# Attention and two MoE layers on one core: the slow widening of one weight unit, shared by VectorE, GpSimd and ScalarE

## The chip, the core and the metric

One core of a Trainium2 chip runs the whole program in one launch. The metric is the device time of that launch in microseconds (us); the kernel before has a median of 787.21 us over three runs (786.08 to 787.22). VectorE is written DVE, ScalarE ACT, GpSimd POOL, TensorE PE, SyncE SP.

## What is computed

```python
def reference(**kwargs):
    attn_out = _attn_ref(q, k, v)             # rotary, softmax(q k^T / 8), times v; (2, 8, 576, 64)
    x = attn_out.transpose(0, 2, 1, 3).reshape(1152, 512)
    x = _moe_ref(x, w_in, w_out)              # silu(x @ w_in) @ w_out, d_ff 2048
    return _moe2_ref(x, domain_probs, w1, w2) # 4 experts: sum_e p_e * relu(x @ w1[e]) @ w2[e]
```

`moe_w_in` and `moe_w_out` come as 8-byte floats. The kernel reads each of them as two 32-bit words, a low word and a high word, and has to build from them a pair of 4-byte tiles whose sum stands for the weight: `wh`, what TensorE multiplies with directly, and `wl`, the rest. Each product is then three matmuls (`wh*xh`, `wh*xl`, `wl*xh`).

## The kernel before

**Attention** works on 8 pairs of heads. A pair has 9 units of work, so that the loop at L1104 takes 72 steps; step i belongs to pair i // 9, and s = i % 9 is its place in the pair. What each step issues on each engine is written out by hand: `PLAN` (L15 to L17) says which background work of the neighbouring pairs falls on which s, and `ORDER` (L18 to L20) in which order a step issues scores (S), row maxima (M), exponentials (E), transposes (T), their evacuations (H on ACT, L on DVE), and the rest. Engines run what they were issued in this order and wait for each other through semaphores. From pair 6 on there is no second pair ahead any more, so that pairs 6 and 7 run by `PLAN2` and `ORDER2` and have no rotary work.

POOL has these steps in each of the pairs 0 to 5: the rotary of the pair after the next (`rotary_k` L232 to L241, `rotary_q` L251 to L267), the low part of V (`vsplit` L284, which waits for ACT's copy at L280), the row factors for the norm (`rbc`, L521 and L526) and the low part of the attention output (`xl`, L550, which waits for ACT's `xh` at L549, which waits for DVE's `xn` at L554).

**The weights.** `Feed` (L119) hands out the widening in stages: each call of `feed.tick` at the end of a step runs one stage of every slice that is under way, then starts another slice if it may (L169, steps in `CONV`, L21). Weight unit 0 (the first 512 columns of `w_in`) is widened during attention, in four slices of 128x512, by `slice0` (L997) with `slow=True`: the slice is loaded into `raw0`, of which there is a single buffer (L156), and then takes one stage in each of nine steps. Slices start at steps 15, 24, 33 and 51, all of them s = 6, so that they lie in pairs 2, 3, 4 and 6. All further units come after attention, or at its very end, in three stages a slice (L117), which the change leaves as they are.

One slice before: ACT takes the absolute value of the high word (t0, L88) and casts `wh` (t5, L104); DVE does the other seven operations (L89, L92, L95, L98, L101, L107, L110). Both words stand interleaved in `raw`, so that `lw` and `hw` are every second 32-bit word.

**The MoE layers** (L882) start in the last pair, run on the tiles `xh` and `xl`, and take the rest of the time.

Of the kernel before, what the change touches and what calls it, by code (L numbers as in the profile page):

```python
# [9 lines left out]
U32 = mybir.dt.uint32  # L10
AF = mybir.ActivationFunctionType
ALU = mybir.AluOpType
# [18 lines left out]
def f32(ap):  # L31
    return ap.bitcast(F32)
# [3 lines left out]
def fused_kernel(ctx, tc, q, k, v, w_in, w_out, dprobs, w1, w2, cst, out):  # L36
    nc = tc.nc
# [43 lines left out]
    def widen(cv, raw, wh, wl, slow=False):  # L81
        lw, hw = (raw.rearrange("p (n a) -> p n a", a=2)[:, :, a] for a in range(2))
        T = {}
        V = nc.vector

        def t0():
            T["t"] = t = cv.tile([128, 512], U32, name="cvt")
            nc.scalar.activation(f32(t), f32(hw), AF.Abs)  # L88
            V.tensor_scalar(lw, lw, 9, None, ALU.logical_shift_right)  # L89

        def t1():
            V.scalar_tensor_tensor(lw, hw, 23, lw, ALU.logical_shift_left, ALU.bitwise_or)  # L92

        def t2():
            V.tensor_scalar(f32(T["t"]), f32(T["t"]), 2.0 ** -15, None, ALU.max)  # L95

        def t3():
            V.tensor_scalar(T["t"][:], T["t"][:], 3, 0x3FFFF000, ALU.logical_shift_left, ALU.bitwise_and)  # L98

        def t4():  # L100
            V.scalar_tensor_tensor(T["t"][:], hw, 0xC0000000, T["t"][:], ALU.bitwise_and, ALU.bitwise_or)  # L101

        def t5():
            nc.scalar.copy(wh, f32(T["t"]))  # L104

        def t6():
            V.tensor_scalar(hw, T["t"][:], 0xFF800000, None, ALU.bitwise_and)  # L107

        def t7():
            V.scalar_tensor_tensor(wl, lw, 2.0 ** -43, f32(hw), ALU.mult, ALU.mult)  # L110

        def together(*fns):
            return lambda: [fn() for fn in fns]

        if slow:
            return [lambda: None, t0, t1, t2, t3, t4, t5, t6, t7]
        return [together(t0, t1), together(t2, t3, t4), together(t5, t6, t7)]  # L117

    class Feed:  # L119
# [722 lines left out]
    def queue(n):  # L842
        wh, wl = wslot[n % 4]
        raws = {}

        def conv(t):
            if t % 2 == 0:
                raws[0] = stg.tile([128, 2, 1024], U32, name="raw", tag="raw")
                nc.sync.dma_start(raws[0][:], units[n][:, t:t + 2, :])
            return widen(cv, raws[0][:, t % 2, :], wh[:, t, :], wl[:, t, :])  # L850

        for t in range(FT):
            feed.add(n, lambda t=t: conv(t))
# [115 lines left out]
    def attention():  # L969
# [27 lines left out]
        def slice0(t):  # L997
            raw = stg0.tile([128, 1024], U32, name="raw0")
            nc.sync.dma_start(raw[:], units[0][:, t, :])
            return widen(cv0, raw, wslot[0][0][:, t, :], wslot[0][1][:, t, :], True)  # L1000
# [274 lines left out]
```

## Time and profile before

| | us |
|---|---|
| median of three runs | 787.21 |
| the profiled execution | 785.77 |
| its span, first to last instruction | 784.0 |
| PE, DVE, ACT, POOL busy in the span | 749.1, 526.2, 349.8, 299.4 |

The profiled execution is 1.44 us below the median; 1.77 us of it lie around the span. A timeline row gives the start of an instruction (or of a run of equal ones, "x2"), its length, and in brackets how long its engine was idle before it and for whom. "POOL xl L550 <- ACT xh L549" says that POOL stood still until ACT had written `xh`. A row of the view by tile gives the shortest, median and longest length of one instruction in ns. The granted clock of TensorE is 0.991 of the full rate over the span and 1.00 in every stretch that is discussed here.

### The profile page before, as it was taken

Reading aid. Unit: us, or ns where it says so; the run is one execution under the profiler, and the core shown is the slowest. Engines: PE = TensorE matmul, PEld = TensorE weight load, DVE = VectorE, ACT = ScalarE, POOL = GpSimd, SP = SyncE. Lnnn points to the kernel's source line nnn. Section 1 sums busy time; section 2 is a strip of 40 time slices with the busy share of each in tenths; the row PEclk is TensorE's granted clock in tenths of the full one; section 3 lists DMA queues with packets and bytes.
Section 4 is the critical chain, followed back from the end, with each engine's and each line's share of the span. In section 5 each row is a group of like instructions: output and inputs, shape, how many; then the busy total and the mean of one; then the engine's idle time right before and its main releaser. Section 6 shows DMA issues by size and latency. Waiting matters only on the chain.

```text
span 784.0 us, 12147 instructions
## 1 busy us (share of the span) xinstructions
PE 749.1 (96%) x4592; PEld 693.9 (89%) x4592; DVE 526.2 (67%) x963; ACT 349.8 (45%) x837; POOL 299.4 (38%) x321
## 2 busy tenths in 40 slices
PE   4898898999999999999969999999999999999998
PEld 3897787989999999999969898988989889898996
DVE  6779998887999899894894454544545454354542
ACT  3788778885534525234443141322423234142320
POOL 8778667521001303105771523516134160432500
PEclk9899999999999999999989999999999999999999
DMA  4443543240313133131100120301103021030002
GB/s 127 117 127 83 127 127 89 63 129 11 103 60 109 54 108 108 55 109 53 54 19 37 42 66 1 108 1 55 55 0 109 0 56 52 3 106 1 1 28 94
DMA packets 30986, 51.89 MB, mean 66 GB/s; under 512 B 7168, under 2 KB 13968, under 8 KB 30928
## 3 DMA queue, kind: packets, MB, share of 16 engines
q1 hardware_dynamic: 28800, 50.06, 21.0%
q10 hardware_dynamic: 2000, 0.77, 0.4%
q8 instruction: 36, 0.59, 0.3%
q0 software_dynamic: 128, 0.28, 0.1%
q14 instruction: 22, 0.18, 0.1%
HBM read 41.40 MB, written 2.36 MB: 56 GB/s over the span
## 4 chain that ended last, share of the span: by engine, by line
PE 83%; DVE 9%; ACT 3%; DMA 2%; issue 1%; POOL 1%; ACTq 0%; DVEq 0%; POOLq 0%
PE m L817 9%; PE m L816 9%; PE m L818 9%; PE m L743 7%; PE m L745 7%; PE m L744 7%; PE m L639 4%; PE m L641 4%; PE m L640 4%; PE b L301 4%; PE b L501 4%; PE m L664 4%; PE m L662 4%; PE m L663 4%; PE s L396 3%; ACT p L425 2%
## 5 line engine op out<-in xcount | busy, mean ns | idle before, releaser
L822 DVE SCALAR_TENSOR_TENSOR acc<-m,dp,acc 128x512 f32<-128x512 f32 (+1 forms) x64 | 47.5, 743 | 112.3 <-PE m L818 112.3
L817 PE MATMUL m<-wl,gh 128*128 128x512 f32 (+1 forms) x292 | 114.6, 392 | 0.0
L818 PE MATMUL m<-wh,gl 128*128 128x512 f32 (+1 forms) x292 | 114.5, 392 | 0.0
L816 PE MATMUL m<-wh,gh 128*128 128x512 f32 (+1 forms) x292 | 114.5, 392 | 0.0
L764 DVE SCALAR_TENSOR_TENSOR gl<-g,gh 128x288 fp32r<-128x288 f32 x96 | 56.9, 593 | 49.1 <-ACT gh L763 48.5
L726 POOL TENSOR_TENSOR wl<-raw,wh 128x512 fp32r<-128x512 f32 x24 | 31.1, 1296 | 142.6 <-ACT wh L723 142.6
L651 POOL TENSOR_TENSOR gl<-g,gh 128x384 fp32r<-128x384 f32 x24 | 27.1, 1130 | 142.3 <-ACT gh L650 142.2
L743 PE MATMUL m<-xh,wh 128*128 128x288 f32 x256 | 76.1, 297 | 0.0
L745 PE MATMUL m<-xh,wl 128*128 128x288 f32 x256 | 75.7, 296 | 0.0
L744 PE MATMUL m<-xl,wh 128*128 128x288 f32 x256 | 75.7, 296 | 0.0
L726 POOL TENSOR_TENSOR wl<-cvt,wh 128x512 fp32r<-128x512 f32 x32 | 41.8, 1309 | 74.0 <-ACT wh L723 74.0
L663 PE MATMUL m<-gh,wl 128*128 128x384 f32 (+1 forms) x208 | 67.2, 323 | 0.0
L664 PE MATMUL m<-gl,wh 128*128 128x384 f32 (+1 forms) x208 | 67.2, 323 | 0.0
L662 PE MATMUL m<-gh,wh 128*128 128x384 f32 (+1 forms) x208 | 67.2, 323 | 0.0
L818 PEld LDWEIGHTS m<-wh,gl 128*128 128x128 f32 x292 | 54.8, 188 | 12.9
L816 PEld LDWEIGHTS m<-wh,gh 128*128 128x128 f32 x292 | 54.9, 188 | 11.9
L817 PEld LDWEIGHTS m<-wl,gh 128*128 128x128 f32 x292 | 54.8, 188 | 11.8
L743 PE MATMUL m<-tf,wh 128*128 128x288 f32 x192 | 57.4, 299 | 6.7 <-DVE g L798 5.6
L723 ACT CAST wh<-cvt 128x512 fp32r<-128x512 f32 x32 | 19.9, 620 | 96.3 <-DVE cvt L722 96.3
L301 PE MATMUL b<-cs,p 128*128 128x128 f32 x329 | 51.1, 286 | 11.0 <-ACT p L1018 7.1
L425 ACT ACTIVATE p<-s,nm 128x576 f32<-128x576 f32 x72 | 53.9, 749 | 9.2 <-DVE nm L415 8.5
L763 ACT ACTIVATE gh<-g 128x288 fp32r<-128x288 f32 x96 | 42.9, 447 | 33.6 <-DVE g L798 19.0
(174 smaller groups left out, 2124.3 us busy)
## 6 DMA issues: line engine op xcount, KB each, us to landing
raw<-in_moe_w_dram SPq DMA_DIRECT2D x16, 1024.0 KB, 5.2
raw<-in_moe_w_out_dram SPq DMA_DIRECT2D x8, 1024.0 KB, 4.9
raw<-in_moe_w_in_dram SPq DMA_DIRECT2D x6, 1024.0 KB, 5.0
kh<-kkh SPq DMA_DIRECT2D x28, 128.0 KB, 2.5
kl<-kkl SPq DMA_DIRECT2D x28, 128.0 KB, 2.4
xv<-in_v_dram SPq DMA_DIRECT2D x8, 256.0 KB, 2.8
raw<-in_moe_w_in_dram SPq DMA_DIRECT2D x4, 512.0 KB, 4.1
xk<-in_k_dram SPq DMA_DIRECT2D x7, 256.0 KB, 2.9
```

Source lines behind the costliest of these rows:

```text
L301: nc.tensor.matmul(o, lhsT, idn[:, 0:n], is_transpose=True, start=True, stop=True)
L425: nc.scalar.activation(o.rearrange("p (a b) -> p a b", a=2), s[:, :, 0:288], AF.Exp, bias=P.nm[:, c:c + 1], scale=1.0, accum_out=P.sm[:, c ...
L662: nc.tensor.matmul(o, wh[:, f, ds], gh[:, cols], start=(f == 0), stop=False)
L663: nc.tensor.matmul(o, wl[:, f, ds], gh[:, cols], start=False, stop=False)
L664: nc.tensor.matmul(o, wh[:, f, ds], gl[:, cols], start=False, stop=(f == FT - 1))
L726: nc.gpsimd.tensor_tensor(lo, src(name), f32(hi), ALU.subtract)
L743: nc.tensor.matmul(ps, wh[:, k, ms], hh[:, k, cols], start=(first and k == 0), stop=False, skip_group_check=not first)
L744: nc.tensor.matmul(ps, wh[:, k, ms], hl[:, k, cols], start=False, stop=False, skip_group_check=not first)
L745: nc.tensor.matmul(ps, wl[:, k, ms], hh[:, k, cols], start=False, stop=(k == 1), skip_group_check=not first)
L816: nc.tensor.matmul(ps, gh[:, ts], wh[:, f, ds], start=(f == 0), stop=False)
L817: nc.tensor.matmul(ps, gh[:, ts], wl[:, f, ds], start=False, stop=False)
L818: nc.tensor.matmul(ps, gl[:, ts], wh[:, f, ds], start=False, stop=(f == FT - 1))
```

## The change

Only the slow form of `widen` changes. New stages u0 to u8 stand beside the old ones; t4 (L101) is kept and called from u3.

```diff
+        def u0():
+            T["t"] = t = cv.tile([128, 512], U32, name="cvt")
+            nc.scalar.activation(f32(t), f32(hw), AF.Abs)
+        def u1():
+            nc.gpsimd.tensor_scalar(f32(T["t"]), f32(T["t"]), 2.0 ** -15, 0.0, ALU.max, ALU.max)
+        def u3():
+            nc.scalar.activation(f32(lw), lw, AF.Copy, scale=2.0 ** -52)
+            t4()
+        def u2():
+            V.tensor_scalar(T["t"][:], T["t"][:], 3, 0x3FFFFFFF, ALU.logical_shift_left, ALU.bitwise_and)
+        def u4():
+            V.tensor_scalar(hw, T["t"][:], 0xFF800000, None, ALU.bitwise_and)
+        def u5():
+            nc.gpsimd.tensor_tensor(f32(hw), f32(lw), f32(hw), ALU.mult)
+        def u6():
+            nc.gpsimd.tensor_tensor(f32(T["t"]), f32(T["t"]), f32(hw), ALU.add)
+        def u7():
+            nc.scalar.copy(wh, f32(T["t"]))
+        def u8():
+            nc.gpsimd.tensor_tensor(wl, f32(T["t"]), f32(wh), ALU.subtract)
         if slow:
-            return [lambda: None, t0, t1, t2, t3, t4, t5, t6, t7]
+            return [lambda: None, u0, u1, u2, u3, u4, u5, u6, u7, u8]
```

For a slice DVE goes from seven operations to three (u2, t4, u4), ACT from two to three (u0, u3, u7), POOL from none to four (u1, u5, u6, u8). There are ten stages instead of nine. Counted from a slice's start, u0 falls on s = 8, u1 on s = 0 of the next pair, u2 on 1, u3 with t4 on 2, u4 on 3, u5 on 4, u6 on 5, u7 on 6, u8 on 7. All other instructions keep their order; their line numbers are 29 higher in the changed kernel.

POOL in pair 2, s = 3 to s = 8, before (`yq` and `t_994` are the rotary's, `xl` the low part of the attention output, `rb` the row factors, `V` the low part of V):

```order
L251 TENSOR_TENSOR t_994<-xq,cs 128x576
L550 TENSOR_TENSOR xl<-xn,xh 128x320
L521 TENSOR_SCALAR rb<-rs 128x256
L254 TENSOR_TENSOR yq<-xq,cs 128x9x64
L258 TENSOR_TENSOR t_994<-t_994,yq 128x576
L264 TENSOR_SCALAR yq<-t_994 128x9x64
L267 TENSOR_TENSOR yq<-t_994,yq 128x9x64
L284 TENSOR_TENSOR V<-xv,V 128x4x64 x2
```

The same place of the changed kernel, from its `yq` of L283 (L254 before) on:

```order
L283 TENSOR_TENSOR yq<-xq,cs 128x9x64
L133 TENSOR_TENSOR raw_766<-raw_766 128x512
L287 TENSOR_TENSOR t_994<-t_994,yq 128x576
L136 TENSOR_TENSOR cvt<-cvt,raw_766 128x512
L293 TENSOR_SCALAR yq<-t_994 128x9x64
L296 TENSOR_TENSOR yq<-t_994,yq 128x9x64
L142 TENSOR_TENSOR wl_65<-cvt,wh_64 128x512
L313 TENSOR_TENSOR V<-xv,V 128x4x64 x2
```

u5 (L133) and u6 (L136) stand behind `xl`, `rb` and two rotary instructions of the same pair, and u8 (L142) behind the last of them.

ACT in pair 2, s = 6 to s = 8, in the changed kernel (`pth` are transposed probabilities, `p,sm` the exponentials, `tmp` a half of the output):

```order
L492 CAST pth<-b 128x4x128
L139 CAST wh_64<-cvt 128x512
L492 CAST pth<-b 128x4x128
L494 COPY p_999<-b 128x128
L454 ACTIVATE p,sm_111<-s,nm 128x576
L377 ACTIVATE Q<-b 128x512
L540 COPY tmp<-b 64x256
L454 ACTIVATE p,sm_112<-s,nm 128x576
L492 CAST pth<-b 128x4x2x64
L494 COPY p_999<-b 128x64
L309 CAST V<-xv 128x4x64 x2
L117 ACTIVATE cvt<-raw_1084 128x512
```

The cast of `wh`, u7 (L139), now stands here between two casts of `pth`, and it needs what POOL's u6 wrote; before, it stood in s = 4 behind the cast of `xh`, and needed DVE's L101.

## Rows read from the trace of the kernel before

**Rows 1.** Windows: stretch, us, then busy us of each engine, clock, DMA share, GB/s.
```profile
58.55:128.32 69.77, 61.00 (x441) 53.94 (x441) 65.71 (x112) 55.16 (x142) 48.14 (x54) 1.00 0.39 99
81.89:105.24 23.35, 20.18 (x148) 17.91 (x148) 21.62 (x38) 18.42 (x48) 16.05 (x19) 1.00 0.42 107
128.32:147.86 19.54, 19.22 (x148) 17.92 (x146) 15.48 (x30) 17.12 (x47) 15.30 (x20) 1.00 0.35 97
147.86:168.52 20.66, 19.75 (x149) 18.03 (x148) 19.45 (x38) 18.37 (x49) 4.92 (x9) 1.00 0.27 66
186.00:784.00 598.00, 587.63 (x3441) 547.87 (x3439) 368.26 (x686) 205.33 (x464) 180.37 (x165) 0.99 0.17 54
```
**Rows 2.** Instructions on tile raw, 57 to 170 us: ns min/median/max, first and last start.
```profile
L88 ACT ACTIVATE cvt<-raw x4: 678/688/702, 58.7 to 148.0; 128x512 f32<-128x512 f32 x4
L89 DVE TENSOR_SCALAR raw<-raw x4: 449/740/789, 59.5 to 148.8; 128x512 uint32<-128x512 uint32 x4
L92 DVE SCALAR_TENSOR_TENSOR raw<-raw x4: 681/888/905, 61.8 to 151.5; 128x512 uint32<-128x512 uint32 x4
L101 DVE SCALAR_TENSOR_TENSOR cvt<-raw,cvt x4: 658/910/1162, 70.1 to 159.0; 128x512 uint32<-128x512 uint32 x4
L107 DVE TENSOR_SCALAR raw<-cvt x4: 417/1584/1600, 74.5 to 163.0; 128x512 uint32<-128x512 uint32 x4
L110 DVE SCALAR_TENSOR_TENSOR wl<-raw x4: 681/1211/1212, 77.5 to 165.1; 128x512 fp32r<-128x512 uint32 x4
```
**Rows 3.** The same view of tile cvt.
```profile
L95 DVE TENSOR_SCALAR cvt<-cvt x4: 407/540/1033, 64.9 to 153.8; 128x512 f32<-128x512 f32 x4
L98 DVE TENSOR_SCALAR cvt<-cvt x4: 417/524/774, 67.1 to 156.7; 128x512 uint32<-128x512 uint32 x4
L104 ACT CAST wh<-cvt x4: 613/614/624, 71.6 to 159.7; 128x512 fp32r<-128x512 f32 x4
```
**Rows 4.** The chain that ended last, 78 to 210 us: start, us, what.
```profile
78.76 4.37 DMA raw<-in_moe_w_in_dram
...
102.10 4.12 DMA raw<-in_moe_w_in_dram
```
**Rows 5.** DVE, timeline: `xn` in pair 3 and in pair 5, and pair 5's longest stop.
```profile
94.05 0.47 DVE L554 TENSOR_TENSOR xn<-xu,b 128x320 f32<-128x320 f32 x1
...
135.98 0.49 DVE L513 TENSOR_TENSOR xu<-b,tmp 64x320 f32<-64x320 f32 x1 [1.29 <-ACT tmp L511]
...
138.20 0.46 DVE L554 TENSOR_TENSOR xn<-xu,b 128x320 f32<-128x320 f32 x1
```
**Rows 6.** POOL, timeline, pair 3.
```profile
81.89 1.43 POOL L284 TENSOR_TENSOR V<-xv,V 128x256 fp32r<-128x256 f32 x2 [3.71 <-ACT V L280]
...
84.18 1.27 POOL L232 TENSOR_TENSOR t<-xk,cs 128x512 f32<-128x512 f32 x1
...
88.53 1.48 POOL L232 TENSOR_TENSOR t<-xk,cs 128x512 f32<-128x512 f32 x1
...
95.09 0.86 POOL L550 TENSOR_TENSOR xl<-xn,xh 128x320 fp32r<-128x320 f32 x1 [1.51 <-ACT xh L549]
95.92 0.40 POOL L521 TENSOR_SCALAR rb<-rs 128x256 f32<-128x256 f32 x1
96.29 1.41 POOL L254 TENSOR_TENSOR yq<-xq,cs 128x576 f32<-128x576 f32 x1
97.78 1.42 POOL L258 TENSOR_TENSOR t<-t,yq 128x576 f32<-128x576 f32 x1
99.28 0.73 POOL L264 TENSOR_SCALAR yq<-t 128x576 fp32r<-128x576 f32 x1
```
**Rows 7.** ACT, timeline, pair 5, s = 6 to s = 8.
```profile
142.69 1.08 ACT L463 CAST pth<-b 128x512 fp32r<-128x512 f32 x2 [0.30 <-PE b L301]
...
145.67 0.36 ACT L511 COPY tmp<-b 64x256 f32<-64x256 f32 x1 [0.51 <-PE b L501]
...
147.35 0.73 ACT L280 CAST V<-xv 128x256 fp32r<-128x256 f32 x2
```

## The prediction

> **What bounds the kernel now.** I read the windows view first, by pairs of heads. The borders are the starts of POOL's low part of V (the two-instruction row at 81.89 in [rows 6]), which comes once a pair, at s = 0. The three widening pairs 2 to 4 last 69.77 us together, 23.26 each; pair 5, with the same work but no widening beyond one load, lasts 19.54; pair 6, with the fourth slice but no rotary, 20.66 [rows 1]. So a slice costs 3.72 us in each of pairs 2 to 4, and about 1.1 in pair 6: some 12 us of attention are what the change can move. In pairs 2 to 4 DVE is busy 65.71 of 69.77, PE 61.00, and POOL 48.14. In pair 5 PE is busy 19.22 of 19.54, and DVE only 15.48 [rows 1]. So DVE bounds the widening pairs, and PE the others. From 186 us on PE is busy 587.63 of 598.00 [rows 1] with nothing to wait for in attention: what attention gains or loses moves the end by as much.
>
> The views by tile show why a slice is dear on DVE. The same instruction has two lengths: L107 takes 417 ns where POOL is quiet (pair 6) and 1584 to 1600 in pairs 2 to 4; L110 681 and 1211, L95 407 and up to 1033, L101 658 and up to 1162 [rows 2, 3]. DVE instructions with both ends in SBUF wait for POOL there. The third thing is in the chain: the single `raw0` buffer is free only when L110, the last stage, has run, so the next slice's load stands on the chain with 4.37 and 4.12 us [rows 4].
>
> **What the change removes.** DVE loses four of seven operations in a pair: L89, L92, L95, L110, at medians 0.74 + 0.89 + 0.54 + 1.21 = 3.4 us. `raw0` is now free after u6, one stage earlier. If nothing came in their place, pairs 2 to 4 would fall towards pair 5's 19.54.
>
> **What it adds.** POOL gets u1 (like L264, 0.73 for 576 columns, so about 0.65), and u5, u6, u8, two-input work on 512 columns like L232 (1.27 to 1.48) [rows 6]: 4.5 us on top of some 16. That still fits into 23 us; the question is where the four stand, because POOL runs in order, and now ACT and DVE wait for it in the middle of a pair. I follow one pair from T0, the start of V on POOL.
>
> *T0 to `xn`.* `xn` of the second half stands in s = 4. In pair 5 it starts 138.20 - 128.32 = 9.88 after T0, in pair 3, with the slice, 94.05 - 81.89 = 12.16 [rows 1, 5, 6]. To pair 5's 9.88 I add: u2 and t4, 0.42 + 0.66 alone to 0.77 + 1.16 beside POOL, against a stop of DVE of 1.29 just behind them (it waits for ACT's `tmp`) [rows 2, 3, 5]: 0 to 0.65 remain, I take 0.1. u0 and u3 on ACT, 0.69 each by L88 [rows 2]; no row shows an in-place activation on integers, L88 is nearest; ACT has 2.4 us idle in pair 5 [rows 1]: 0 to 1.4, I take 0.3. u4, directly in front of `xn` on DVE, 0.42 to 1.58 as L107 [rows 2]: I take 0.9, since POOL's rotary may or may not run just then. Sum 11.2; ends 10.3 and pair 3's own 12.16, where DVE had more to do. u1 finishes about 2.3 + 1.3 + 1.0 = 4.6 after T0 (the start of the first L232, its length, then a short rotary instruction and u1 [rows 6]). DVE came to L95, where u2 now stands, 64.9 - 58.55 = 6.3 after T0 in pair 2 [rows 1, 3], with the 1.6 of L89 and L92 in front of it that now go: 4.7. So no stall is booked there, but there is no room either.
>
> *`xn` to u6.* `xl` starts 95.09 - 94.05 = 1.04 behind `xn`. Then POOL runs `xl` 0.83 (start to start), `rb` 0.37, L254 1.41, u5 1.27, L258 1.42, u6 1.27 = 6.57 [rows 6]. u5 reads and writes every second word; no POOL row has that, so its ends are 1.27 and 1.48 plus a tenth, the tenth being what L88, which reads so, takes beyond L104, which doesn't (688 and 614 ns [rows 2, 3]). I take 1.27.
>
> *u6 to the next T0.* ACT comes to u7 between two casts of `pth`. In pair 5 that place is at 142.69 + 0.5 = 143.2, which is 5.0 behind `xn` [rows 5, 7]. u6 ends 1.04 + 6.57 = 7.6 behind `xn`. **So ACT stands still for 2.6 us at u7**, with the second cast, the exponentials and V queued behind it; PE and DVE run dry soon after. From u7 on ACT has, by pair 5, 147.86 - 143.2 = 4.66 to the next T0, less 0.51 of waiting for PE that is over by then, plus u7's 0.62: 4.77 [rows 1, 3, 7]. The next load, issued behind u6, lands 4.37 later [rows 4], just ahead of u0; so the load leaves the chain, with half a microsecond to spare.
>
> Period: 11.2 + 1.04 + 6.57 + 4.77 = 23.6, against 23.26: +0.3 a pair, +1.0 over three. What DVE gives up comes back as ACT's wait for POOL.
>
> *Pair 6.* POOL is free (4.92 busy), so u6 is there in time. DVE is busy 19.45 of 20.66 and loses at least 2.2 by the shortest lengths; PE's idle time, 20.66 - 19.75 = 0.9, caps the gain [rows 1, 2, 3]. 0 to -0.9, I take -0.5.
>
> **Sum:** +1.0 - 0.5 = +0.5. The profiled execution has 785.77 us, span 784.0 and 1.77 around it; it becomes 786.3. The median of the runs lies 1.44 higher, so I forecast **787.7**.
>
> **Ends.** Low: `xn` at 10.3, period 22.7, -1.7 over three pairs, -0.9 in pair 6: 784.6. High: `xn` at 12.16, u5 and u6 0.2 longer each, period 24.95, +5.1, pair 6 at 0: 792.3.
>
> **Rivals.**
> *POOL holds ACT longer (slower).* The two bit operations t4 and u4 meet POOL's rotary at full length, which delays `xn`, and u5 and u6 start later and run longer. For it: L107 and L110 at 1.58 and 1.21 in just these pairs [rows 2], and POOL's 1.48 where 1.27 would do [rows 6]. Against: in s = 1 to 3 DVE has fewer such operations than before. That is the high end, 792; it counts as slower, by over 0.2% (1.57 us, about what a measurement of this kernel tells from no change), from a period of 23.95, so from `xn` at 11.6. The Trainium skill, "SBUF — State Buffer", section "Who interferes with whom", says more: the loser of the port that VectorE and GpSimd share is blocked for the whole instruction of the other. By that rule u4 could cost 1.42 + 0.42 = 1.84, not 0.9, and the sum would be 790.5. The trace agrees in kind (1584 against 417 ns), though it shows 1.17 of waiting and not 1.42.
>
> *POOL isn't late (faster).* If u6 were done when ACT comes to u7, the period would be 11.2 + 5.0 + 4.77 = 21.0, -6.9 in all with pair 6 at -0.5 on top: 779.8. For it: POOL is idle a quarter of each widening pair. Against: that idle time lies in front of V and of `xl` ([rows 6], 3.71 and 1.51), where it doesn't help u6; even without u5 and u6 the four instructions from `xl` to L258 take 4.03, which leaves nothing of ACT's 5.0 less 1.04. The Trainium skill speaks against it as well: "GPSIMD Engine Reference", section "Engine selection", keeps two-input elementwise work on VectorE, GpSimd being some 2 times slower; the trace agrees, 1.27 against 0.68 for L110 alone.
>
> *A milder gain.* The ends of `xn` and of pair 6 near their low values: 784.6 to 785.6. For it: the load leaves the chain, and DVE has 3.4 us less to do in front of and behind `xn`.
>
> **How the numbers follow.** Forecast, within 0.2%: 0.43. Slower by over 0.2% (the first rival, and the upper part of the forecast's own terms): 0.35. Faster by over 0.2%: 0.22, of which 0.05 for POOL not late, the rest for the milder gain. The range leaves out the strong gain and the tip of the slow rival: 784.4 to 791.5.
>
> **What would show it.** After: DVE's busy share in pairs 2 to 4 clearly down (65.71 to about 58), POOL's up by some 13 us. A new wait, ACT `wh` for POOL `cvt`, of 2 to 3 us in each of pairs 2 to 4 and near none in pair 6. No load of `raw` in the chain, POOL's L254, u5, L258, u6 there instead, in one run. `xn` 11 us behind T0, periods of 23 to 24, pair 6 about 20.2. Wrong it would be if that wait were under 1 us (then the gain rival), if DVE waited at u2 for u1 (POOL late from the pair's start), or if u5 and u6 took much over 1.3 us each.

## The result and the profile after

| | before | after |
|---|---|---|
| median, us (9 runs each, side by side) | 785.40 | 789.22 |
| ratio after / before, 95% interval | | 1.0054 [1.0036, 1.0073] |
| profiled execution, us | 785.77 | 792.44 |
| its span, us | 784.0 | 790.7 |
| pairs 2, 3, 4, us | 23.34, 23.35, 23.08 | 23.81, 24.52, 24.46 |
| pair 5, pair 6, us | 19.54, 20.66 | 20.90, 20.34 |
| the five pairs together, us | 109.97 | 114.03 |

The change makes the kernel slower by 0.5%: some 4.2 us by the ratio (0.0054 of 785.4), and 4.06 us by the five pairs of the profiled executions. Those two agree, and the place is found: pairs 2 to 4 lose 3.02, pair 5 loses 1.36, pair 6 gains 0.32. The spans differ by more, 6.7 us. 1.92 of that is the start up to T0 of pair 2 (58.55 before, 60.47 after), in which no changed instruction runs; over the profiles of all the kernels here it lies anywhere between 54.8 and 60.8 us. So kernels are compared below by the stretch from T0 of pair 2 to T0 of pair 7, and a median may carry a microsecond or two of that start. The mean granted clock of the nine executions after lies between 0.984 (three of them, the profiled one included, 792.2 to 792.6 us) and 0.996 (789.01 us), and the median one has 0.993; since one of the three falls described below lowers that mean by 0.002, and profiles without them have up to 0.996 (experiment 1), the median has room for one at most. What those falls cost is therefore read for the profiled execution.

First the page of the kernel after: busy time of each engine (share of the span, instructions).

```profile
PE 752.5 (95%) x4592; PEld 697.7 (88%) x4592; DVE 517.0 (65%) x947; ACT 352.5 (45%) x841; POOL 319.4 (40%) x337
```

DVE lost 9 us over the span and POOL gained 20, as meant. Busy time was never the question; the windows view of the kernel after shows it (columns as in [rows 1]: stretch, us, busy of PE, PEld, DVE, ACT, POOL, then TensorE's clock, DMA share, GB/s). The rows are pairs 2 to 4, pair 3 alone, pair 5, pair 6, and the stretch after attention.

```profile
60.47:133.26 72.79, 63.14 (x432) 56.69 (x432) 54.80 (x98) 56.94 (x145) 62.84 (x67) 0.93 0.38 95
84.28:108.80 24.52, 21.46 (x146) 19.32 (x145) 18.06 (x34) 19.02 (x49) 20.95 (x22) 0.92 0.41 102
133.26:154.16 20.90, 20.57 (x156) 19.28 (x155) 16.70 (x31) 17.24 (x47) 15.38 (x20) 0.99 0.36 91
154.16:174.50 20.34, 19.64 (x148) 17.84 (x147) 17.66 (x34) 18.83 (x50) 10.20 (x12) 1.00 0.28 67
192.56:790.70 598.14, 587.71 (x3438) 547.94 (x3436) 368.35 (x684) 205.69 (x464) 180.29 (x165) 0.99 0.16 54
```

Against [rows 1]: in pairs 2 to 4 DVE falls from 65.71 to 54.80, and POOL rises from 48.14 to 62.84. None of the engines is full. Two things are new: the clock, 0.93 in the widening pairs where it was 1.00, and pair 5, which holds no slice and yet takes 1.36 longer. After attention nothing has changed: 587.71 of 598.14.

The view of waits of the same kernel, 60.47 to 133.26 (total, times, longest):

```profile
DVE ptl L497 <- ACT pth L492: 10.4, 9, 2.9
...
ACT wh L139 <- POOL cvt L136: 7.6, 3, 2.5
PE b L330 <- ACT p L454: 6.6, 4, 2.2
```

The middle row is the wait that the prediction named, once a pair, 2.5 each. The first and the last are what stands behind it: DVE waits for ACT's `pth`, and PE for the exponentials. The chain of the same kernel, end of pair 3 (start, us, what), shows what ACT waited for:

```profile
97.26 0.47 ACT xh L578
...
97.80 0.86 POOL xl L579
98.66 0.37 POOL rb L550
99.03 1.40 POOL yq L283
100.43 1.00 POOL raw L133
101.43 1.38 POOL t L287
102.81 1.26 POOL cvt L136
...
104.12 0.50 issue
104.61 0.58 ACT pth L492
```

Six POOL instructions run without a gap between `xh` and u7 (L139, at 104.09), where the load and DVE's widening stood before [rows 4]. The timelines at the ends of pairs 3 and 2 show how this goes on to ACT, and to PE:

```profile
100.98 0.59 ACT L492 CAST pth<-b 128x512 fp32r<-128x512 f32 x1 [0.30 <-PE b L330]
104.09 0.62 ACT L139 CAST wh<-cvt 128x512 fp32r<-128x512 f32 x1 [2.52 <-POOL cvt L136]
104.61 0.58 ACT L492 CAST pth<-b 128x512 fp32r<-128x512 f32 x1
```

```profile
78.88 0.59 PE L530 MATMUL b<-p,v 128*128 128x256 f32 x2
81.63 0.66 PE L330 MATMUL b<-cs,p 128*128 128x128 f32 x4 [2.16 <-ACT p L454]
...
83.89 1.06 PE L330 MATMUL b<-cs,p 128*128 128x128 f32 x4
```

PE stands still for 2.16 us, about as long as ACT. Then its own work takes longer: four transposes in 0.66 right after the stop, the same four in 1.06 two microseconds later. Windows of 1 us over that place tell why (the number behind POOL's is the clock):

```profile
81.00:82.00 1.00, 0.37 (x3) 0.37 (x4) 1.00 (x2) 1.00 (x3) 1.00 (x2) 1.00 0.93 238
82.00:83.00 1.00, 1.00 (x10) 0.77 (x9) 0.49 (x2) 0.95 (x3) 0.89 (x1) 0.83 0.89 340
83.00:84.00 1.00, 1.00 (x6) 0.98 (x6) 0.29 (x1) 1.00 (x5) 0.00 (x0) 0.50 0.68 201
84.00:85.00 1.00, 1.00 (x7) 1.00 (x6) 0.97 (x2) 1.00 (x4) 0.72 (x2) 0.50 0.14 28
85.00:86.00 1.00, 1.00 (x6) 0.98 (x6) 0.50 (x4) 1.00 (x3) 1.00 (x3) 0.50 0.00 0
86.00:87.00 1.00, 1.00 (x9) 1.00 (x8) 1.00 (x3) 0.78 (x3) 1.00 (x3) 0.96 0.20 23
```

PE stops at about 79.5 and is busy again from 81.6. From about 82.7 to 86 the granted clock is 0.50 (1.2 of 2.4 GHz), and PE, busy throughout, gets through 6 or 7 instructions in each microsecond instead of 9 or 10. The same comes behind the other two stops: 0.50 from about 106.6 to 110, and from about 130.5 to 133.9, some 3.4 us each time. T0, which hangs on ACT, is reached at 84.28, 108.80 and 133.26 all the same, before PE has caught up; the work that PE is then behind with falls into the next pair. The Trainium skill, "TensorE: Matmul & The Clock Gate", section "HAM oscillation — how this bites in real kernels", describes such a pattern for waits for loads: the wait recurs in each round of a loop, and TensorE starts each round at half rate. The trace agrees in kind: three stops of 2.16 or 2.17 us, and 0.50 behind each. But here PE waits for ACT and not for a load, and at the first stop the clock falls only at 82.7, a microsecond after PE is busy again.

### The profile page after: what moved, and what is told of

It is laid out like the page before. It is cut to its first block, busy times and chain, and to the rows that moved or that the text cites. A ratio compares the mean times of both kernels' runs of the same rounds, so it can differ in the third digit from the quotient of the medians.

```text
span 790.7 us, 12145 instructions
## 1 busy us (share of the span) xinstructions
PE 752.5 (95%) x4592; PEld 697.7 (88%) x4592; DVE 517.0 (65%) x947; ACT 352.5 (45%) x841; POOL 319.4 (40%) x337
## 4 chain that ended last, share of the span: by engine, by line
PE 84%; DVE 6%; ACT 4%; POOL 4%; issue 1%; DMA 1%; SPq 0%; ACTq 0%; POOLq 0%; DVEq 0%
PE m L846 9%; PE m L845 8%; PE m L847 8%; PE m L772 7%; PE m L774 7%; PE m L773 7%; PE b L330 4%; PE m L668 4%; PE m L670 4%; PE m L669 4%; PE b L530 4%; PE m L693 4%; PE m L691 4%; PE m L692 4%; PE s L425 3%; ACT p L454 2%
## 5 line engine op out<-in xcount | busy, mean ns | idle before, releaser
L846 PEld LDWEIGHTS m<-wl,gh 128*128 128x128 f32 x292 | 54.8, 188 | 11.8
L444 DVE TENSOR_REDUCE nm<-s 128x1 f32<-128x576 f32 x72 | 53.8, 748 | 9.9 <-PE s L425 7.3
L497 DVE TENSOR_TENSOR ptl<-b,pth 128x512 fp32r<-128x512 f32 x72 | 49.2, 687 | 16.8 <-ACT pth L492 16.0
```

The costliest lines, as they stand in the source:

```text
L846: nc.tensor.matmul(ps, gh[:, ts], wl[:, f, ds], start=False, stop=False)
```

## The experiments

Theory A: the loss is ACT's wait at u7 for POOL's u6, together with the fall of TensorE's clock behind the stop that this wait makes in PE. Theory B: the loss comes from the first half of a pair, where POOL has u1 more to do and DVE's operations meet POOL's. All ratios are to the kernel before, run on the same chip alongside, with 95% intervals. The order of the pairs' lengths is 2, 3, 4 | 5 | 6, then the sum's difference to the 109.97 before.

| kernel | ratio | pairs, us | difference |
|---|---|---|---|
| after | 1.0054 [1.0036, 1.0073] | 23.81, 24.52, 24.46, then 20.90, then 20.34 | +4.06 |
| 1: u7 one step later | 0.9969 [0.9951, 0.9986] | 22.43, 23.64, 23.60, then 19.53, then 20.26 | -0.51 |
| 2: u7 two steps later | 0.9938 [0.9915, 0.9962] | 21.20, 22.40, 22.39, then 19.89, then 20.25 | -3.84 |
| 3: PE kept busy | 1.0011 [0.9998, 1.0023] | 23.86, 23.80, 23.81, then 19.67, then 20.34 | +1.51 |
| 4: u1 on DVE | 1.0034 [1.0016, 1.0053] | 23.80, 24.54, 24.44, then 20.94, then 20.18 | +3.93 |
| 5: POOL one product longer | 1.0068 [1.0049, 1.0087] | 24.78, 25.49, 26.74, then 20.97, then 20.82 | +8.83 |
| 6: as 2, two load buffers | 0.9945 [0.9923, 0.9967] | 21.18, 22.39, 22.36, then 19.82, then 20.24 | -3.98 |
| 7: as 6, u1 on DVE | 0.9899 [0.9877, 0.9920] | 21.16, 20.93, 20.93, then 19.84, then 20.10 | -7.01 |
| 8: as 6, u1 as max and mult | 0.9960 [0.9931, 0.9990] | 21.19, 22.37, 22.39, then 19.84, then 20.26 | -3.92 |
| 9: before, two load buffers | 0.9995 [0.9978, 1.0012] | 23.32, 23.09, 23.05, then 19.54, then 20.66 | -0.31 |
| 10: as 7, one load buffer | 0.9940 [0.9920, 0.9960] | 21.17, 22.65, 22.65, then 19.85, then 20.12 | -3.53 |

**1. u7 one step later.**

```diff
-            return [lambda: None, u0, u1, u2, u3, u4, u5, u6, u7, u8]
+            return [lambda: None, u0, u1, u2, u3, u4, u5, u6, lambda: None, u7, u8]
```

> The changed kernel with one empty stage ahead of u7, so that the cast of wh stands one place later on ScalarE, behind the second cast of pth, the copy and one exponential (about 1.36 us of work that no longer stands behind the wait). Theory A (the loss is ScalarE's wait for GpSimd's u6, 2.52 us in each of pairs 2 to 4, and the fall of TensorE's clock that follows it): the wait falls to about 1.2 us, TensorE's stop to under 1 us, and with it the clock's fall goes or shortens; periods of pairs 2 to 4 from 24.3 to about 22.5; time about 0.998 of the kernel before. Theory B (the loss is GpSimd's greater load and the port that it shares with VectorE, in the first half of a pair): nothing changes there, 1.004 to 1.006 as with the change.

The empty stage moves u7 and u8 behind POOL's step, nothing else. Waits of this kernel, 54 to 175 us:

```profile
ACT wh L139 <- POOL cvt L136: 3.4, 3, 1.2
DVE cvt L127 <- POOL cvt L120: 3.4, 3, 1.5
```

ACT's wait halves, from 2.5 to 1.2. Pair 5, in which this kernel runs what the kernel after runs there and one u8 more (POOL is busy 16.50 us for 15.38), is back at 19.53 from 20.90: its loss belonged to the stall at the end of pair 4 and to nothing in pair 5. What had not been foreseen is the second row. u8 now falls into the next pair, in front of u1 in POOL's order, so u1 ends later and DVE waits for it at u2, which it had hardly done in the kernel after (0.4 in all). Pairs 3 and 4, those that begin with another slice's u8, stay 1.2 longer than pair 2. The stretch gives only 0.51 of the 2.4 us that the ratio stands for (0.0031 of 788); what the rest is, the profile doesn't settle.

**2. u7 two steps later.**

```diff
-            return [lambda: None, u0, u1, u2, u3, u4, u5, u6, u7, u8]
+            return [lambda: None, u0, u1, u2, u3, u4, u5, u6, lambda: None, lambda: None, u7, u8]
```

> Two empty stages ahead of u7: the cast of wh falls on s = 8, some 4 us later on ScalarE than u6 needs. Theory A: no wait of ScalarE for u6, TensorE's clock stays at 1.00, periods of pairs 2 to 4 about 21, pair 5 back to 19.6; time about 0.991 of the kernel before, faster than both kernels. Theory B: 1.004 to 1.006 as with the change.

Waits of this kernel, 54 to 175 us; and its windows row of pair 3:

```profile
ACT cvt L117 <- DMA raw<-in_moe_w_in_dram: 2.1, 2, 1.2
...
DVE cvt L127 <- POOL cvt L120: 0.7, 2, 0.4
```

```profile
79.30:101.70 22.40, 20.07 (x148) 17.97 (x147) 18.56 (x33) 18.88 (x49) 20.90 (x24) 1.00 0.42 111
```

The wait at u7 is gone, the clock is 1.00, and the same ten operations on the same engines are now faster than the kernel before. Theory A holds as to the place: two empty stages turn +4.06 into -3.84. Two smaller things take the wait's place. The load, which the prediction saw leave the chain "with half a microsecond to spare", is late by 1.2 now that ACT comes to u0 sooner. And POOL is busy 20.90 of 22.40.

**3. PE kept busy.** In pairs 2 to 4, 16 matmuls run ahead of one group of `av`, into the same place that the group then overwrites; they are redundant, and everything else is as after.

```diff
+            if i == 0 and (hf, h) == (0, 1) and 2 <= P.n <= 4:
+                for _ in range(16):
+                    nc.tensor.matmul(T["ps"], st, mv, start=True, stop=True)
```

> The changed kernel, with 16 further matmuls (128x256 each, into the same PSUM bank, overwritten by the real ones) on TensorE just ahead of the value product at s = 7 of pairs 2 to 4, where TensorE would stand idle for 2.2 us behind ScalarE's wait. They cost about 2 us of TensorE that the wait hides. Theory A with the clock as its second half: ScalarE's wait stays at 2.5 us, but the clock stays at 1.00 behind it; periods from 24.3 to about 23.2, pair 5 from 20.9 to 19.6; time about 0.9995 to 1.001 of the kernel before. If the clock had no part (A without its second half, or B): no gain, 1.004 to 1.009.

Windows of pairs 2 to 4 and of pair 5, waits, and PE's timeline around pair 2's end:

```profile
58.64:130.11 71.47, 66.06 (x489) 59.62 (x489) 55.97 (x100) 56.72 (x145) 62.90 (x67) 1.00 0.37 97
130.11:149.78 19.67, 19.35 (x147) 17.95 (x147) 15.74 (x30) 17.15 (x47) 15.32 (x20) 1.00 0.35 97
```

```profile
ACT wh L139 <- POOL cvt L136: 7.6, 3, 2.5
```

```profile
76.01 2.15 PE L532 MATMUL b<-pth,V 128*128 128x256 f32 x16
...
79.84 0.66 PE L330 MATMUL b<-cs,p 128*128 128x128 f32 x4 [0.30 <-ACT p L454]
```

This divides theory A into its two halves. ACT's wait is the same 7.6; only PE's stop has shrunk from 2.16 to 0.30, filled with redundant work. The clock stays at 1.00, pairs 3, 4 and 5 become shorter by 0.72, 0.65 and 1.23, and pair 2, ahead of which there is no stall, doesn't (23.86 against 23.81). So in the profiled executions the clock costs 2.6 of the 4.06 us, all of it in the pair after a stall; with the clock held, the change costs +1.51. By the ratios the filling gives back 0.0043, with intervals that don't meet; against experiment 4's kernel, whose pairs are as long as after's, the medians on the same chip are 788.37 and 789.61, only 1.2 us apart. How much of the clock is in a median stays open.

With the clock held one can also see where the +1.51 lies. From T0 to `xn` this kernel takes 11.78, 11.73 and 11.74 us in pairs 2 to 4, the kernel before 12.13, 12.16 and 11.88. From `xn` to the next T0, where u5, u6 and the wait at u7 stand, it takes 12.07 or 12.08, and the kernel before 11.19 to 11.21. The second half of a pair loses 0.87, and the first half gains 0.1 to 0.4.

**4. u1 on DVE.**

```diff
-            nc.gpsimd.tensor_scalar(f32(T["t"]), f32(T["t"]), 2.0 ** -15, 0.0, ALU.max, ALU.max)
+            V.tensor_scalar(f32(T["t"]), f32(T["t"]), 2.0 ** -15, None, ALU.max)
```

> The changed kernel with u1, the maximum, back on VectorE (0.4 us there alone) in place of GpSimd, where it takes 1.92 us. Theory A: the wait at u7 stays at about 2.5 us, since u1 lies ahead of where GpSimd stands idle for xl; time within 0.3% of the change, 1.003 to 1.007 of before. Theory B: GpSimd is rid of 1.9 us a pair and VectorE of its wait at u2; 1.5 us a pair come back, 0.999.

u1 is POOL's longest new instruction: the view by tile of the kernel after (ns shortest/median/longest, first and last start) has it at 1.92 us, three times what the prediction booked for it.

```profile
L120 POOL TENSOR_SCALAR cvt<-cvt x4: 1922/1925/1930, 64.1 to 156.3; 128x512 f32<-128x512 f32 x4
L127 DVE TENSOR_SCALAR cvt<-cvt x4: 924/942/970, 66.1 to 159.5; 128x512 uint32<-128x512 uint32 x4
L101 DVE SCALAR_TENSOR_TENSOR cvt<-raw,cvt x4: 681/792/798, 68.2 to 163.0; 128x512 uint32<-128x512 uint32 x4
L130 DVE TENSOR_SCALAR raw<-cvt x4: 399/919/1051, 71.3 to 165.5; 128x512 uint32<-128x512 uint32 x4
```

Taking it away from POOL changes none of the pairs 2 to 5 by more than 0.04. The 1.5 us a pair that theory B expected don't come back, and by experiment 3 the first half of a pair is no longer than before, so theory B doesn't account for the loss. But that does not make u1 free on POOL. In pair 2 of the kernel after DVE waits for it, and the chain from T0 to `xn` runs through it. DVE's timeline of that pair (`xu` is the output ahead of the norm):

```profile
66.08 0.97 DVE L127 TENSOR_SCALAR cvt<-cvt 128x512 uint32<-128x512 uint32 x1 [0.36 <-POOL cvt L120]
...
69.06 0.49 DVE L542 TENSOR_TENSOR xu<-b,tmp 64x320 f32<-64x320 f32 x1
...
72.24 0.48 DVE L583 TENSOR_TENSOR xn<-xu,b 128x320 f32<-128x320 f32 x1
```

In experiment 4 that wait is gone, but in pair 2 DVE's own u1 takes 1.20 and u4 1.38, and `xn` comes 72.31 - 60.57 = 11.74 us after T0 in place of 72.24 - 60.47 = 11.77. So the experiment shows that u1 costs the same in either place, and not that it costs nothing.

**5. POOL one product longer.** A product whose result `wl` is overwritten later runs ahead of u6, 1.04 us each.

```diff
+            nc.gpsimd.tensor_tensor(wl, f32(lw), f32(hw), ALU.mult)
             nc.gpsimd.tensor_tensor(f32(T["t"]), f32(T["t"]), f32(hw), ALU.add)
```

> The changed kernel with one more two-input instruction on GpSimd directly ahead of u6 (a product into wl, which u8 overwrites): the suspected wait made longer. Theory A: ScalarE's wait at u7 grows by that instruction's length, from 2.5 to 3.5 to 3.8 us in each of pairs 2 to 4, and near nothing in pair 6; periods from 24.5 to about 25.6; time about 1.009 to 1.010 of before. If the loss came from elsewhere, it is as with the change, 1.004 to 1.006.

Waits of this kernel, over the same pairs:

```profile
ACT wh L140 <- POOL cvt L137: 10.9, 4, 3.5
```

The longest wait grows by 1.0, from 2.5 to 3.5, for 1.04 us more on POOL: each microsecond there is one of ACT's. Pairs 2 to 4 become longer by 0.97, 0.97 and 2.28; in the last the clock has a part, since it stands at 0.50 from 104.0, in the stop at the end of pair 3, to about 110.8, twice as long as in the kernel after. The stretch is 4.8 us longer than after's, yet the ratio is only 0.0014 higher (1.1 us). That size isn't settled; the profiled execution reached T0 of pair 2 at 56.94, 3.5 us earlier than that of the kernel after.

**6. Two load buffers on top of 2.**

```diff
-    stg0 = apool(lctx, "stg0", 1, "left")
+    stg0 = apool(lctx, "stg0", 2, "left")
```

> e2_late2 with two buffers for raw0, so that the load of the next slice no longer waits for u6. In e2_late2 ScalarE still waits 2.1 us in two places for that load, and pairs 3 and 4 (22.4 us) are 1.2 longer than pair 2 (21.2). Theory A: that is the load alone; the wait goes, pairs 3 and 4 fall to about 21.2 to 21.6, and the time by some 2 us, to 0.991 of before. If GpSimd itself bounds these pairs by now (20.9 us busy of 22.4): they stay at 22 and above, 0.994.

Theory A's expectation failed. The wait for the load is gone, but the pairs stay where they were; waits of this kernel:

```profile
DVE cvt L127 <- POOL cvt L120: 3.1, 3, 1.4
```

The next wait has grown from 0.7 to 3.1: ACT's u0 is earlier, and POOL's u1 isn't (it starts 4.87 after T0 in pair 3, 4.89 in experiment 2), because POOL works without a stop from T0 to u1's end, with u8 in between. So POOL seems to hold pairs 3 and 4 here, and the load's 1.2 us lay beside POOL's work; experiment 7 tries that.

**7. The same with u1 on DVE** (the lines of 4 and 6 on top of 2).

> e6 with u1, the maximum, on VectorE. Where GpSimd bounds a pair, its 1.92 us now count (they did not in e4, where GpSimd stood idle ahead of xl): pairs 3 and 4 fall to 20.5 to 21, 0.988 to 0.990 of before. If GpSimd doesn't bound them: as e6, within 0.2%.

Windows of pairs 2 to 4 and of pair 5:

```profile
56.20:119.22 63.02, 59.66 (x440) 54.00 (x440) 56.43 (x102) 55.83 (x144) 56.91 (x62) 1.00 0.42 110
119.22:139.06 19.84, 19.52 (x147) 18.04 (x147) 15.93 (x30) 17.64 (x48) 16.54 (x21) 1.00 0.36 96
```

Pairs 3 and 4 come down to 20.93, with PE busy 59.66 of 63.02. This version beats both kernels, at 778.61 us and 0.9899 [0.9877, 0.9920]. Moving u1, worth nothing in experiment 4, is worth 3.0 us of the stretch here: what a move gives depends on which engine is awaited at that place.

**8. u1 as maximum and product,** on top of 6, to see whether two maxima in one instruction make it long.

```diff
-            nc.gpsimd.tensor_scalar(f32(T["t"]), f32(T["t"]), 2.0 ** -15, 0.0, ALU.max, ALU.max)
+            nc.gpsimd.tensor_scalar(f32(T["t"]), f32(T["t"]), 2.0 ** -15, 1.0, ALU.max, ALU.mult)
```

> e6 with u1 as maximum and then times 1.0 in place of a second maximum with 0.0, the same values. If the 1.92 us of u1 come from the maximum itself, it stays near 1.9; if from the pair of maxima, it falls towards the 0.65 that a multiply pair takes on GpSimd, and the time goes with e7.

```profile
L120 POOL TENSOR_SCALAR cvt<-cvt x4: 1921/1928/1933, 58.5 to 142.7; 128x512 f32<-128x512 f32 x4
```

It stays 1.93 us in this kernel's view by tile: one maximum is enough to make it that long.

**9. The kernel before with two load buffers** (the line of 6 in the old kernel).

> The kernel before with two buffers for raw0 and nothing else. ScalarE and VectorE waited for that load up to 1.0 us at the start of pairs 3 and 4. If that wait was the bound there, pairs 3 and 4 fall by about 1 us each, 0.997 to 0.998 of before; if VectorE's seven operations were, the wait only moves and nothing changes, 0.999 to 1.001. Either way it tells how much of e6 is the buffer, and not the sharing of the work.

0.9995, no difference, though the load stood in the old chain with 4.37 and 4.12 us [rows 4]. DVE, busy 65.71 of 69.77 there [rows 1], is next behind it: the chain names the last to arrive, not by how much.

**10. Experiment 7 with one load buffer.**

> e7 without the second raw0 buffer: u7 two stages later and u1 on VectorE, one buffer. If the buffer matters once GpSimd no longer bounds the pairs, ScalarE waits again about 1 us for the load at the start of pairs 3 and 4, and the time is about 2 us above e7's, 0.992 of before; if not, 0.990.

```profile
ACT cvt L117 <- DMA raw<-in_moe_w_in_dram: 2.3, 2, 1.1
```

Pairs 3 and 4 go from 20.93 to 22.65, and ACT waits for the load again. The second buffer, worth nothing in 6 and 9, is worth 3.5 us of the stretch once neither POOL nor DVE is late behind it. Experiments 6, 7 and 10 belong together: two limits of nearly the same height, of which either hides the other.

## Why the prediction was right, and where it was wrong

The time lies in the range, and the kernel is slower, which the prediction had as its second likeliest outcome behind no change. The wait at u7 was right in place and size. That the range covers the time is in part luck: its upper end was drawn for a later `xn`, longer u5 and u6 and nothing from pair 6. u5 and u6 weren't longer, pair 6 did gain, and `xn` passed 12.16 only behind the fall of the clock, which was in neither end. The difference is further off than the time: +0.5 forecast and +3.8 measured between the medians, because the kernel before had 785.40 beside the kernel after, and not the 787.21 that the forecast started from. Point by point:

- **ACT's stop at u7**, "2.6 us": 2.52 in pair 3, 7.6 over the three pairs, none in pair 6. Right, in place and size; experiments 2 and 5 show that it is a cause and not only a sign.
- **`xn` to u6 and on to T0**, 1.04 + 6.57 + 4.77: in pair 3 `xl` begins 97.80 - 96.75 = 1.05 behind `xn`, u6 ends 104.06 - 97.80 = 6.26 later, and the next T0 is 108.80 - 104.09 = 4.71 behind u7. 0.33 less in all, most of it because u5 takes 1.03 and not 1.27, as POOL's timeline of pair 3 shows:

```profile
97.80 0.86 POOL L579 TENSOR_TENSOR xl<-xn,xh 128x320 fp32r<-128x320 f32 x1 [1.25 <-ACT xh L578]
...
100.40 1.03 POOL L133 TENSOR_TENSOR raw<-raw 128x512 f32<-128x512 f32 x1
...
102.77 1.29 POOL L136 TENSOR_TENSOR cvt<-cvt,raw 128x512 f32<-128x512 f32 x1
```

- **T0 to `xn`**, "sum 11.2": mis-sized. `xn` comes 72.24 - 60.47 = 11.77 behind T0 in pair 2, and 11.73 in pair 3 of experiment 3, where the clock is held. Most of it is there by `xu`, which starts 69.06 - 60.47 = 8.59 after T0 in pair 2, against 135.98 - 128.32 = 7.66 in pair 5 before [rows 1, 5]: 0.93 later, where 0.1 for u2 and t4 and 0.3 for u0 and u3 were booked. Two terms are at fault, u2, which takes 0.94 (L127 under experiment 4) where 0.42 to 0.77 was read [rows 3], and the wait for u1, which was booked as none. From `xu` to `xn` 3.18 - 2.22 = 0.96 was added, where 0.9 was booked for u4; u4 took 0.92. By the rule of the Trainium skill that stood beside it ("SBUF — State Buffer", section "Who interferes with whom") it could have cost 1.84; in the kernel after it took 1.05 at most, against 0.40 alone, so the rows were the nearer guide. In pair 3 of the kernel after, `xn` comes later still, by DVE's timeline 96.75 - 84.28 = 12.47 behind T0; the 0.7 more are the clock's.

```profile
96.75 0.47 DVE L583 TENSOR_TENSOR xn<-xu,b 128x320 f32<-128x320 f32 x1
```

- **The step that failed** is the one behind the stop: "PE and DVE run dry soon after". The prediction saw PE stop, and then went on with every duration at full clock and with pair 5 as before. In the profiled execution each stop of 2.16 us is followed by some 3.4 us at half clock, and what that costs falls into pairs 3, 4 and 5: 0.72 + 0.65 + 1.23 = 2.6 us by experiment 3.
- **The sum**, +0.5: measured +4.06 between the profiled executions. The clock is 2.6 of the difference; `xn`, 0.57 later in each of three pairs, less the 0.33 behind it (12.04 from `xn` to T0 in pair 2, booked at 12.38), is 0.7; pair 5 without the clock 0.1; pair 6, forecast at -0.5, gave -0.32, which is another 0.2. That makes 3.6.
- **u1**, "about 0.65": 1.92, wrong by a factor of three. "So no stall is booked there" failed with it: u1's end came 5.6 after T0 and not 4.6, DVE was at u2 in pair 2 after 66.08 - 0.36 - 60.47 = 5.25, and stood still for 0.36. That is the prediction's own sign of POOL being late from the pair's start, in small. In pair 3 of the kernel after, behind the fall of the clock, DVE came to u2 only 90.63 - 84.28 = 6.35 after T0 and did not wait; with the clock held (experiment 3) it waited in all three pairs, 1.4 us in all.
- **The load**, out of the chain "with half a microsecond to spare": right for the kernel after, where ACT never waited for it.
- **The rivals.** The slower one held by its sign, and only in small part by its mechanism: `xn` was half a microsecond later than booked, but u5 and u6 didn't run longer, and in the profiled execution the larger part was the clock, which it didn't have. "POOL isn't late" (779.8) fell, but a good half of what it priced was there: experiment 2 lets ACT ask for u6 later instead of POOL making it sooner, and pairs 2 to 4 lose 3.8 of the 6.9 us, with a ratio of 0.9938.

## What to carry to other kernels

When an in-order engine is made to wait, follow the stop to TensorE and price the time behind it as well: here, in the profiled execution, 2.6 of 4.06 us were lost to half clock behind gaps of 2.2 us, and showed up in the pair after each. Where stages are handed out by a table, try first to move the consumer of a late result: two empty stages were worth 7.9 us of the stretch with every operation left on its engine. And an instruction, a buffer or a load that costs nothing in one experiment may be worth 3 us once the limit beside it is gone, so the two are to be tried together.

## What the runs showed of the hardware

- A maximum on POOL is slow: 1.92 us for 128x512 four-byte elements, with one maximum or two, where a POOL product by numbers takes 0.67 on 128x576 (L293). On DVE the same maximum had a median of 0.58 in experiment 4.
- POOL's in-place product of every second word (u5, 1.03) is faster than its sum of a dense tile and every second word (u6, 1.29), of the same 128x512. Working in place isn't the reason: experiment 5's product of the same two operands into the dense `wl` takes 1.04. Whether it is the operation or the operands stays open.
- TensorE's clock fell to 0.50, for some 3.4 us, behind each of the stops of 2.16 or 2.17 us in the profile of the kernel after, though not in every execution of that kernel. In experiment 2 PE stopped for 1.12 and the clock stayed at 1.00.
